# Fourth chunk: the third softmax group takes the slots of the first behind the softmax turns; two GpSimd memsets trade places

## The chip, the cores and the metric

The kernel runs on one NeuronCore of a Trainium2 chip (trn2), the seven other cores idle. The metric is device time in microseconds (us) of one execution. Before the change the median of three runs is 240.81 us (240.27 to 241.5). Smaller is better.

## The reference

Sinkhorn-sorted block attention, followed by a feed-forward layer with the activation h cos(h). Cut to what matters:

```python
# q, k, v: (4, 8, 768, 64); sort_net: (4, 8, 8, 8); w_in: (512, 2048); w_out: (2048, 512)
P = sort_net
for _ in range(5):
    P = exp(P - P.max(-1)); P = P / P.sum(-1); P = P / P.sum(-2)   # (+1e-9 in both sums)
k_sorted = einsum('bhij,bhjcd->bhicd', P, k_blocks)                # 8 blocks of 96 tokens
v_sorted = einsum('bhij,bhjcd->bhicd', P, v_blocks)
s = q_blocks @ k_sorted.T / 8                                      # per block of 96 tokens
attn = softmax(s) @ v_sorted
x = attn.transpose(0, 2, 1, 3).reshape(3072, 512)
h = x @ w_in
out = (h * cos(h)) @ w_out                                         # (3072, 512)
```

## The kernel before, in words

**Tiling.** The 3072 tokens are worked in eight chunks of 384 tokens, n = 0 to 7. A chunk is half a batch entry: four blocks of 96 tokens, which the code calls u = 0 to 3 and this text calls groups. "Fourth chunk" is n = 3, and its "first" and "third" groups are u = 0 and u = 2. The number n also says which buffer of a pair is used: `q_turned[n % 2]`.

**Steps of a group.** `qk n u` makes the scores of all eight heads on TensorE (PE; line 535), from the turned queries and the sorted keys: `kP0` for n = 1, `kP1` for n = 2 and 3, `kPg` from n = 4 on. `mx` takes row maxima off on VectorE (DVE; lines 572, 581). `ex` is the exponential on ScalarE (ACT; line 586), into one of three buffers `p_buf`. `pd` turns (transposes) the probabilities by a DMA on SyncE's queue (SP; line 598) into a tile `pT`; this is the softmax turn. `av` multiplies them with the sorted values on PE (line 617), with a column of ones that gives the softmax sums. `xn` takes the reciprocal of the sums and scales on DVE (lines 627, 629). The result is turned once more into the chunk's tile `xT`, by a DMA on SP (`xd`, line 638) or by PE (`xp`, line 646) and a copy on ACT or DVE.

**The layer.** When all four groups are in `xT`, `up` multiplies with `w_in` (line 661; a call of two 128-column tiles of `w_in` is eight matmuls), `ga` makes h cos(h) by a sine on ACT and a product on DVE (lines 671, 678) and `dn` multiplies with `w_out` (line 694). The `dn` calls of a chunk are laid between the attention steps of the next chunks, where they fill PE. `oc` copies results out of PSUM, `st` stores them by SP.

**Other steps near the change.** `vg` makes sorted values of batch entries 2 and 3 on PE (line 517) and `e vg` copies them out. `qd` turns a chunk's queries by SP (line 439). `z_k g part` is a memset on GpSimd (POOL; line 342) that zeroes one half (64 rows) of one of four slots of a key tile: `z_k 1 2` zeroes rows 64 to 127 of slot 0 of `kP1` (64x768), `z_k 2 1` rows 0 to 63 of slot 2 of `kPg` (64x1536). Before `z_k 1 2` may write, the copy `ksw 1 0` (SP, line 476) must have read that half of slot 0, since it moves it into slot 1. The scores of chunk 2, `qk 2 ...`, read all four slots of `kP1`. `ld_q`, `ld_kg` and `ld_vg` (lines 285, 270, 274) are loads that POOL issues. `v1` makes sorted values of batch entry 1 (line 508); `b_sum`, `b_inv` belong to the Sinkhorn rounds (lines 358, 386).

**What sets the order.** The list `PLAN` is the program order, written out by hand: each string is a call, each call issues instructions on fixed engines, and every engine and queue works through its own in that order (the schedule is manual, so nothing is moved). Waits come from the data that instructions share and from buffers: a name such as `B0` or `C1` at the end of a call is the PSUM pool in which its result lies until it is read. The lines ahead of the change in the fourth chunk:

```python
"pd 3 1", ..., "st 1 2 S", "pd 3 2", "e vg 40 4 A", "pd 3 0", ..., "qd 4", ..., "pd 3 3", "st 2 1 S",
```

So SP turns the groups in the order 1, 2, 0, 3, with the store `st 1 2` behind the first and `qd 4` ahead of the last.

Of the kernel before, what the change touches and what calls it, by code (L numbers as in the profile page):

```python
# [53 lines left out]
    "ex 1 2 0", "ld_q 2 0", "av 1 1 B0", "b_norm 1", "pp 1 2 C0", "dn 0 2 3", "xp 1 0 B2", "qd 2",  # L54
    "b_ci 1", "e pp 1 2 A", "ksw 1 0", "z_k 1 3", "xp 1 3 B1", "xn 1 1", "dn 0 2 0", "b_exp 1",
    "e xp 1 3 V", "av 1 2 B0", "xn 1 2", "xp 1 1 C0", "ld_q 3 2", "v1 40 8 B1", "e xp 1 1 A", "ld_kg 1 2",
    "e xp 1 0 A", "ld_kg 0 2", "dn 0 2 1", "z_k 2 1", "xp 1 2 B0", "e v1 40 8 V", "b_sum 1 C0",
    "e xp 1 2 A", "z_k 1 2", "qk 2 0 0 B2", "ld_q 3 0", "v1 48 8 B1", "b_inv 1", "qk 2 1 0 C0",
    "oc 0 2 V 0", "mx 2 0 0", "e v1 48 8 A", "mx 2 1 0", "up 1 0 2 0 384 B0", "up 1 4 2 0 384 B1",
    "b_norm 1", "ga 1 0 2 0 384", "up 1 6 2 0 384 B2", "up 1 14 2 0 384 B0", "ga 1 4 2 0 384", "st 0 1 S",  # L60
    "qk 2 0 1 C1", "up 1 10 2 0 384 B1", "ga 1 6 2 0 384", "up 1 12 2 0 384 B2", "ld_q 3 1", "mx 2 0 1",
    "ld_q 3 3", "ga 1 14 2 0 384", "ga 1 10 2 0 384", "v1 8 8 C0", "up 1 8 2 0 384 B0",
    "up 1 2 2 0 384 B1", "b_ci 1", "ga 1 12 2 0 384", "ld_vg 2 6", "e v1 8 8 V", "v1 24 8 C1",
# [18 lines left out]
    "dn 2 1 1", "dn 2 1 3", "dn 2 1 2", "mx 3 0 1", "pd 3 1", "mx 3 3 2", "vg 40 4 B0", "ld_q 5 0",  # L82
    "ex 3 0 0", "st 1 2 S", "pd 3 2", "e vg 40 4 A", "pd 3 0", "ld_q 5 3", "vg 48 4 B1", "dn 2 0 0",
    "oc 2 1 V 0", "vg 24 8 B2", "e vg 48 4 A", "dn 2 0 3", "av 3 1 B1", "vg 0 8 B0", "ex 3 3 0",
    "dn 2 2 3 C1", "e vg 24 8 A", "av 3 0 B2", "z_ones 1", "oc 2 0 A 0", "vg 36 4 C0", "e vg 0 8 A",
    "xn 3 1", "dn 2 2 1", "av 3 2 B0", "xn 3 0", "vg 8 8 B1", "qd 4", "dn 2 2 2", "xn 3 2", "e vg 36 4 A",
    "pd 3 3", "st 2 1 S", "av 3 3 B0", "xn 3 3", "e vg 8 8 A", "dn 2 2 0", "oc 2 2 A 0", "xp 3 1 B2",
    "e xp 3 1 V", "vg 32 4 C0", "xd 3 0", "qk 4 0 1 B0", "e vg 32 4 A", "xp 3 3 B1", "vg 16 8 B2",
    "xd 3 2", "e xp 3 3 V", "qd 5", "mx 4 0 1", "qk 4 1 1 C1", "qk 4 1 0 C0", "mx 4 1 1", "e vg 16 8 A",
    "up 3 4 2 0 384 B1", "up 3 6 2 0 384 B2", "mx 4 1 0", "up 3 0 2 0 384 B0", "ga 3 4 2 0 384",  # L90
    "qk 4 0 0 C1", "up 3 2 2 0 384 B1", "ga 3 6 2 0 384", "ga 3 0 2 0 384", "up 3 12 2 0 384 B2",
    "ga 3 2 2 0 384", "up 3 8 2 0 384 B0", "up 3 10 2 0 384 B1", "ga 3 12 2 0 384", "up 3 14 2 0 384 B2",
# [682 lines left out]
```

## Time and profile before

| | |
|---|---|
| median of 3 runs | 240.81 us (240.27 to 241.5) |
| the profiled execution's own time | 240.12 us |
| its span, first to last instruction | 238.3 us |
| PE busy | 229.6 us, 96% |
| VectorE / ScalarE / GpSimd busy | 174.0 / 147.9 / 73.6 us |
| mean granted TensorE clock | 0.997 |

The profile has a page of totals and views of the trace. In the timeline a row is: start, duration (us), engine, line, operation, out<-in and shapes, a count, and in brackets the idle time of the engine ahead of it with what ended it. PE is the matmul itself, PEld its weight load, which runs ahead beside PE. An SPq row is the issuing of a DMA, not its transfer. Matmuls overlap by about 0.2 us, so the distance from start to start tells more than the durations do. In the chain of waits (the work that ended last, followed back) a row is start, duration, what. In the view of DMA issues the last number is the time from the start of an issue to landing.

### The profile page before, as it was taken

The numbers are of one execution on the slowest core, as the hardware profiler recorded it, in microseconds if no ns is written. First come the engines' busy times: TensorE is split into PE (matmuls) and PEld (weight loads), VectorE is DVE, ScalarE is ACT, GpSimd is POOL, SyncE is SP. The second block draws the span as 40 slices with busy tenths as digits, with TensorE's granted clock in tenths as the row PEclk, the third lists the DMA queues.
The fourth block names the chain that finished last, engine by engine and source line by source line (L and its number), as shares of the span: only waits on it lengthen the run. The fifth ranks groups of instructions, "written<-read, shape, count | busy, mean of one in ns | idle before, by whom it ended". The sixth has DMA issues, their size and how long they took to land.

```text
span 238.3 us, 5223 instructions
## 1 busy us (share of the span) xinstructions
PE 229.6 (96%) x2127; PEld 148.3 (62%) x2127; DVE 174.0 (73%) x301; ACT 147.9 (62%) x202; POOL 73.6 (31%) x82
## 2 busy tenths in 40 slices
PE   8998998999999999999899999999999999999994
PEld 5787888966666565655565665555565555555543
DVE  2489967698879975796598888777989967715422
ACT  2346666766487967778486945783777387706420
POOL 8149599730942299930045000000000000000000
PEclk9999999999999999999999999999999999999998
DMA  5999999999999986979669346015731592331202
GB/s 67 232 188 224 200 188 125 157 183 156 200 193 199 178 183 142 154 48 161 162 87 114 57 95 149 12 23 112 192 91 28 139 184 44 94 96 66 110 37 95
DMA packets 67767, 30.78 MB, mean 129 GB/s; under 512 B 57248, under 2 KB 63264, under 8 KB 67488
## 3 DMA queue, kind: packets, MB, share of 16 engines
q0 software_dynamic: 26080, 13.63, 43.5%
q1 hardware_dynamic: 41296, 16.75, 31.1%
q8 instruction: 16, 0.26, 0.4%
q10 hardware_dynamic: 368, 0.07, 0.1%
q14 instruction: 7, 0.06, 0.1%
HBM read 27.27 MB, written 6.29 MB: 141 GB/s over the span
## 4 chain that ended last, share of the span: by engine, by line
PE 76%; DMA 9%; DVE 5%; POOL 4%; ACT 2%; issue 1%; SPq 1%; POOLq 0%; DVEq 0%; ACTq 0%
PE h L661 33%; PE o L694 28%; PE idle L347 4%; DMA w_in_t<-in_moe_w_in_dram 4%; PE sc L535 3%; PE av L617 3%; DMA pT<-p_buf 2%; DMA xT<-xn 2%; SPq L598 1%; DMA kP<-kP 1%; DVE kPg L369 1%; POOL vperm L491 1%; PE vs L517 1%; PE ks L467 1%; PE vs L499 1%
## 5 line engine op out<-in xcount | busy, mean ns | idle before, releaser
L694 PE MATMUL o<-w_out_t,gall 128*128 128x512 bf16 (+2 forms) x400 | 93.6, 370 | 0.1
L661 PE MATMUL h<-xT,w_in_t 128*128 128x384 bf16 (+1 forms) x576 | 86.8, 308 | 1.4 <-DMA w_in_t<-in_moe_w_in_dram 0.7
L678 DVE TENSOR_TENSOR gall<-c,h 128x768 bf16<-128x768 f32 x64 | 60.2, 951 | 25.3 <-ACT c L671 24.8
L671 ACT ACTIVATE c<-h,half_pi 128x768 f32<-128x768 f32 x64 | 57.3, 901 | 28.6 <-PE h L661 27.9
L661 PEld LDWEIGHTS <-w_in_t 128*128 128x128 bf16 x576 | 53.9, 98 | 31.1 <-issue 0.8
L694 PEld LDWEIGHTS <-gall 128*128 128x128 bf16 x400 | 36.2, 98 | 31.1 <-issue 0.4
L491 POOL COPY vperm<-kv 128x1536 bf16<-128x1536 bf16 (+1 forms) x10 | 28.3, 2848 | 10.1 <-PE sc L535 8.7
L586 ACT ACTIVATE p_buf<-s 96x768 bf16<-96x768 f32 x32 | 26.7, 842 | 6.4 <-DVE s L581 3.7
L572 DVE TENSOR_REDUCE mx<-sc 96x4 f32<-96x384 f32 (+1 forms) x39 | 28.1, 719 | 2.5 <-PE sc L535 2.5
L581 DVE TENSOR_TENSOR s<-sc,mx 96x384 f32<-96x384 f32 (+1 forms) x33 | 24.3, 736 | 2.3
L285 POOL DMA_DIRECT2D q_mem<-in_q_dram x24 | 18.5, 779 | 18.9 <-DMA q_turned<-q_mem 18.9
L629 DVE TENSOR_TENSOR xn<-av,r 96x512 bf16<-96x512 f32 x32 | 22.0, 686 | 1.1
L347 PE MATMUL idle<-warm 128*128 128x256 bf16 x109 | 17.4, 296 | 2.3 <-DVE warm L308 1.0
L249 ACT COPY kv<-o 128x512 f32<-128x512 f32 (+1 forms) x13 | 7.2, 557 | 15.6 <-PE o L694 15.6
L347 PEld LDWEIGHTS <-warm 128*128 128x128 bf16 x109 | 10.8, 108 | 5.4 <-DVE warm L308 1.0
L627 DVE RECIPROCAL r<-av 96x8 f32<-96x8 f32 x32 | 6.4, 201 | 10.3 <-PE av L617 9.9
L535 PEld LDWEIGHTS <-q_turned 128*128 128x128 bf16 x112 | 9.7, 100 | 4.5 <-issue 0.5
L249 ACT COPY xT<-xps 128x384 bf16<-128x384 bf16 x9 | 4.2, 479 | 12.3 <-PE xps L646 12.3
L671 ACT ACT_TABLE_LOAD x8 | 10.3, 1283 | 0.1
L617 PEld LDWEIGHTS <-pT 96*128 96x128 bf16 (+1 forms) x160 | 7.6, 101 | 4.0 <-DMA pT<-p_buf 1.4
L249 ACT CAST vS<-vs 96x512 bf16<-96x512 f32 x12 | 6.9, 585 | 5.0 <-PE vs L499 3.6
L249 ACT CAST pair<-vs 96x512 bf16<-96x512 f32 (+1 forms) x11 | 8.0, 746 | 3.2 <-PE vs L517 3.2
(103 smaller groups left out, 207.6 us busy)
## 6 DMA issues: line engine op xcount, KB each, us to landing
out_dram<-kv SPq DMA_DIRECT2D x14, 256.0 KB, 2.4
q_mem<-in_q_dram POOLq DMA_DIRECT2D x24, 96.0 KB, 3.6
out_dram<-o_s SPq DMA_DIRECT2D x9, 256.0 KB, 2.5
w_in_t<-in_moe_w_in_dram POOLq DMA_DIRECT2D x4, 512.0 KB, 11.5
w_out_t<-in_moe_w_out_dram POOLq DMA_DIRECT2D x4, 512.0 KB, 7.4
kv<-in_k_dram POOLq DMA_DIRECT2D x2, 768.0 KB, 8.1
kv<-in_v_dram POOLq DMA_DIRECT2D x2, 768.0 KB, 10.1
kv<-in_v_dram POOLq DMA_DIRECT2D x6, 256.0 KB, 11.0
```

The lines of the kernel that those rows point to most:

```text
L249: A.copy(dst, src)
L285: G.dma_start(out=q_mem[:, n % 2].rearrange("p (i h d) -> p i h d", i=IC, h=H)[:, i], in_=q[b].rearrange("h (i c) d -> i c h d", c=blk)[ih ...
L347: nc.tensor.matmul(idle[:], warm[:], warm[:, :1].to_broadcast([128, 256]), start=True, stop=True)
L491: G.tensor_copy(dst, src)
L572: V.reduce_max(m[:], scv, axis=AX.X)
L581: V.tensor_tensor(dst, scv, m.to_broadcast([blk, w, H2, blk]), op=ALU.subtract)
L586: A.activation(p[:, :, :blk], s_t.pop((n, u)).rearrange("p z a c -> p (z a) c"), AF.Exp, scale=scale)
L629: V.tensor_tensor(x[:], avv[:, :, :, :D], r.to_broadcast([blk, 2, H2, D]), op=ALU.mult)
L661: nc.tensor.matmul(hv[f], w_in_t[:, kk, (f0 + f) * 128:(f0 + f + 1) * 128], x_of(n)[:, kk, lo:hi], start=(kk == 0), stop=(kk == KC - 1))
L671: A.activation(cc, hh, AF.Sin, bias=half_pi[:, 0:1])
L678: V.tensor_tensor(dst, cc, hh, op=ALU.mult)
L694: nc.tensor.matmul(out_ps[key][:], gall[:, g_at(n, f), ts * 128:(ts + 1) * 128], w_out_t[:, f, c], start=(parts[key] == 1 and f == fs[0]), ...
```

## The change

In the fourth chunk, `av 3 0` and `av 3 2` trade places, and with them `xn 3 0` and `xn 3 2`, and `xd 3 0` and `xd 3 2`. The PSUM pools stay with the places: the first of the two uses B2 and the second B0, as before. So the order of `av` goes from 1, 0, 2, 3 to 1, 2, 0, 3. Further up, while chunk 1 is in the attention, `z_k 1 2` is put ahead of `z_k 2 1`. No call is added or taken away. (The other lines of the diff are the same calls wrapped differently.)

```diff
-    "e xp 1 0 A", "ld_kg 0 2", "dn 0 2 1", "z_k 2 1", "xp 1 2 B0", "e v1 40 8 V", "b_sum 1 C0",
-    "e xp 1 2 A", "z_k 1 2", "qk 2 0 0 B2", "ld_q 3 0", "v1 48 8 B1", "b_inv 1", "qk 2 1 0 C0",
+    "e xp 1 0 A", "ld_kg 0 2", "dn 0 2 1", "z_k 1 2", "z_k 2 1", "xp 1 2 B0", "e v1 40 8 V", "b_sum 1 C0",
+    "e xp 1 2 A", "qk 2 0 0 B2", "ld_q 3 0", "v1 48 8 B1", "b_inv 1", "qk 2 1 0 C0", "oc 0 2 V 0",
...
-    "dn 2 2 3 C1", "e vg 24 8 A", "av 3 0 B2", "z_ones 1", "oc 2 0 A 0", "vg 36 4 C0", "e vg 0 8 A",
-    "xn 3 1", "dn 2 2 1", "av 3 2 B0", "xn 3 0", "vg 8 8 B1", "qd 4", "dn 2 2 2", "xn 3 2", "e vg 36 4 A",
+    "dn 2 2 3 C1", "e vg 24 8 A", "av 3 2 B2", "z_ones 1", "oc 2 0 A 0", "vg 36 4 C0", "e vg 0 8 A",
+    "xn 3 1", "dn 2 2 1", "av 3 0 B0", "xn 3 2", "vg 8 8 B1", "qd 4", "dn 2 2 2", "xn 3 0", "e vg 36 4 A",
     "pd 3 3", "st 2 1 S", "av 3 3 B0", "xn 3 3", "e vg 8 8 A", "dn 2 2 0", "oc 2 2 A 0", "xp 3 1 B2",
-    "e xp 3 1 V", "vg 32 4 C0", "xd 3 0", "qk 4 0 1 B0", "e vg 32 4 A", "xp 3 3 B1", "vg 16 8 B2",
-    "xd 3 2", "e xp 3 3 V", "qd 5", "mx 4 0 1", "qk 4 1 1 C1", "qk 4 1 0 C0", "mx 4 1 1", "e vg 16 8 A",
+    "e xp 3 1 V", "vg 32 4 C0", "xd 3 2", "qk 4 0 1 B0", "e vg 32 4 A", "xp 3 3 B1", "vg 16 8 B2",
+    "xd 3 0", "e xp 3 3 V", "qd 5", "mx 4 0 1", "qk 4 1 1 C1", "qk 4 1 0 C0", "mx 4 1 1", "e vg 16 8 A",
```

4 rows, old and new, of the table PLAN are left out of this document.

## The prediction, made before the result was known

> **What bounds the kernel now.** I read the page first, for the engine that fills the span, and its slices.
>
> ```profile
> PE 229.6 (96%) x2127; PEld 148.3 (62%) x2127; DVE 174.0 (73%) x301; ACT 147.9 (62%) x202; POOL 73.6 (31%) x82
> ```
>
> TensorE is busy for 229.6 of 238.3 us, so a change that removes no matmul can win only where PE stands still. The list of who waited for whom says where, and the chain of waits whether such a place sets the end. Two places belong to the edits. In the first, between 56 and 65 us, the chain leaves PE and runs through a copy of keys and GpSimd's queue, and comes back to PE with the scores of chunk 2:
>
> ```profile
> 56.05 3.32 DMA kP<-kP
> ...
> 62.08 1.39 POOL kPg L342
> ...
> 63.52 0.74 POOL kP L342
> ...
> 64.31 0.32 PE sc L535 x2
> ```
>
> The reader is to see that the 1.39 us of `z_k 2 1` stand on the chain ahead of `z_k 1 2`, though the scores read only what `z_k 1 2` zeroes. In the second place the chain leaves PE for a softmax turn:
>
> ```profile
> 109.41 4.64 DMA pT<-p_buf
> ```
>
> This is `pd 3 0`, the third turn of chunk 3, which lands at 109.41 + 4.64 = 114.05; `av 3 0`, second of its chunk on PE, waits for it. Elsewhere the chain is matmuls nearly throughout, with short DMA turns that themselves begin at a PE result. Between the two places PE hardly ever rests, as the view of stretches shows for 60 to 92 us (length, then PE's busy time):
>
> ```profile
> 60.00:92.00 32.00, 31.59 (x304) 20.25 (x302) 25.55 (x48) 23.34 (x36) 20.08 (x18) 1.00 1.03 180
> ```
>
> With 31.59 us of 32 busy, time won at the first place should be kept by what follows.
>
> **Edit one, the two memsets.** The timeline there:
>
> ```profile
> 59.51 0.73 POOL L342 MEMSET kP<- 64x768 f32 x1 [9.25 <-DMA kP<-kP]
> ...
> 62.05 1.42 POOL L342 MEMSET kPg<- 64x1536 f32 x1
> ...
> 63.15 0.68 DVE L251 CAST vS<-vs 96x512 bf16<-96x512 f32 x1
> ...
> 63.52 0.73 POOL L342 MEMSET kP<- 64x768 f32 x1
> 63.54 0.35 PE L358 MATMUL sk<-E,kPg 128*128 128x8 f32 x2
> ...
> 63.74 0.48 ACT L249 COPY xT<-xps 128x384 bf16<-128x384 bf16 x1 [0.41 <-PE xps L646]
> 63.94 0.21 DVE L386 RECIPROCAL rr<-sk 128x8 f32<-128x8 f32 x1
> ...
> 64.21 2.34 POOL L285 DMA_DIRECT2D q_mem<-in_q_dram  x3
> 64.31 0.32 PE L535 MATMUL sc<-kP,q_turned 128*128 128x192 bf16 x2 [0.41 <-POOL kP L342]
> ...
> 64.47 0.40 PE L508 MATMUL vs<-kPg,vperm 128*128 128x64 bf16 x8
> ...
> 64.70 0.33 PE L535 MATMUL sc<-kP,q_turned 128*128 128x192 bf16 x2
> ...
> 64.87 5.36 PE L661 MATMUL h<-xT,w_in_t 128*128 128x384 bf16 x32
> ```
>
> The bracket says that PE stood 0.41 us for `z_k 1 2`. How early can that memset run? It must wait for the copy `ksw 1 0`, issued by SP at 59.14 and landing 3.6 us later:
>
> ```profile
> 59.14 0.69 SPq L476 DMA_DIRECT2D kP<-kP  x1
> ```
>
> ```profile
> kP<-kP SPq DMA_DIRECT2D x1, 192.0 KB, 3.6
> ```
>
> That is 62.74. The other copy landed at 56.05 + 3.32 = 59.37 and its memset began at 59.51, so 0.14 us later; `z_k 1 2` can begin at 62.88, not at 62.05. In the trace of before its start and the start of the scores are 64.31 - 63.52 = 0.79 apart; so the zeros allow the scores at 62.88 + 0.79 = 63.67. PE itself reaches them about 0.15 behind the small fp32 pair, estimated from the same pair at its earlier place, ahead of `av`:
>
> ```profile
> 57.62 0.28 PE L358 MATMUL sk<-E,kPg 128*128 128x8 f32 x2
> ...
> 57.77 0.42 PE L617 MATMUL av<-vS,pT 96*128 96x65 bf16 x8
> ```
>
> So 63.54 + 0.15 = 63.69, and the memset is just in time: the first scores gain 64.31 - 63.69 = 0.62. What is late next? Taking 0.06 from a finished instruction to the one it releases (the memset's 63.52 + 0.73 = 64.25 against 64.31): `v1 48 8`, 0.16 behind the scores, would go at 63.85, and its pool B1 is free when the cast at 63.15 ends, 63.83 + 0.06 = 63.89. `qk 2 1 0` would follow 0.23 later, at 64.12, but its pool C0 is read by the reciprocal `b_inv` until 63.94 + 0.21 = 64.15, so 64.21. The first `up` comes 0.17 behind, at 64.38; its `xT` is copied by 63.74 + 0.48 = 64.22. Against 64.87 that is **0.49 us** won. Bounds: 0 from below if something else holds the scores to 64.31, 0.62 from above if both pools let go early.
>
> [...]
>
> What the edit pushes back: POOL now idles from 62.07 to 62.88, so `z_k 2 1` runs at about 63.6 to 65.0 and everything POOL issues behind it comes about 0.8 later: `ld_q 3 0`, `3 1`, `3 3`, then three `ld_vg`, up to a fourth that waits for an older load until 71.32 anyway:
>
> ```profile
> 71.32 0.53 POOL L274 DMA_DIRECT2D kv<-in_v_dram  x1 [3.14 <-DMA pair<-in_k_dram]
> ```
>
> ```profile
> 81.21 1.40 SPq L439 DMA_TRANSPOSE q_turned<-q_mem  x1
> ```
>
> ```profile
> q_mem<-in_q_dram POOLq DMA_DIRECT2D x1, 96.0 KB, 11.0
> ```
>
> The last query load (issued until 64.21 + 2.34 = 66.55, 11.0 to landing) is there before 77.6, by 78.4 after the change, and `qd 3` uses it at 81.21: nearly 3 us of cover. POOL stood 3.14 us ahead of 71.32, which takes up the 0.8, so the last `ld_vg`, and the copies `vp` that need all of them, keep their time. The first user of `z_k 2 1` itself is the copy `ksw 2 1`, behind `qd 3` in the plan. I cost all of this at nothing; if the cover were gone, PE would wait by what is missing, at most the 0.8.
>
> **Edit two, the fourth chunk.** SP turns groups 1, 2, 0, 3, but PE asks in the order 1, 0, 2, 3:
>
> ```profile
> 108.05 2.60 SPq L598 DMA_TRANSPOSE pT<-p_buf  x2
> ...
> 112.13 1.03 PE L694 MATMUL o<-w_out_t,gall 128*128 128x512 bf16 x4
> ...
> 112.83 1.24 SPq L598 DMA_TRANSPOSE pT<-p_buf  x1
> 114.10 0.32 PEld L617 LDWEIGHTS <-pT 96*128 96x128 bf16 x8 [1.44 <-DMA pT<-p_buf]
> 114.11 0.43 PE L617 MATMUL av<-vS,pT 96*128 96x65 bf16 x8 [0.95 <-DMA pT<-p_buf]
> 114.16 0.53 SPq L709 DMA_DIRECT2D out_dram<-o_s  x1
> ...
> 114.60 1.03 PE L694 MATMUL o<-w_out_t,gall 128*128 128x512 bf16 x4
> ...
> 115.46 0.42 PE L617 MATMUL av<-vS,pT 96*128 96x65 bf16 x8
> 115.53 2.52 SPq L638 DMA_TRANSPOSE xT<-xn  x2
> ...
> 117.03 0.42 PE L617 MATMUL av<-vS,pT 96*128 96x65 bf16 x8
> ...
> 119.78 4.06 PE L661 MATMUL h<-xT,w_in_t 128*128 128x384 bf16 x24
> ```
>
> ```profile
> pT<-p_buf SPq DMA_TRANSPOSE x1, 3.7
> ```
>
> ```profile
> pT<-p_buf SPq DMA_TRANSPOSE x1, 3.1
> ```
>
> (The first is `pd 3 2`, the second `pd 3 3`.) From 114.60 to 115.46, four `dn` matmuls take 0.86 from start to start; without a wait `av` would have begun at 112.13 + 0.86 = 112.99. So the stall is 114.11 - 112.99 = 1.12, more than the 0.95 of the bracket, which counts from a modelled end.
>
> After the change that place holds `av 3 2`, whose turn landed at 108.05 + 3.7 = 111.75, more than 1 us ahead. The 1.12 falls away. The next place, now `av 3 0`, would begin at 115.46 - 1.12 = 114.34; its turn lands at 114.05, good from 114.11: 0.23 to spare. The third, `av 3 3`, would begin at 117.03 - 1.12 = 115.91, but its turn lands at 112.83 + 3.1 = 115.93, so it begins at 115.99. What is left of the gain is 117.03 - 115.99 = **1.04 us**. That small wait is what is late next.
>
> The moved `xd` calls: SP is free after the store at 114.16 + 0.53 = 114.69. `xd 3 2` goes then instead of at 115.53, `xd 3 0` behind it, 1.26 later (half of 2.52), at about 116.0, and lands 2.3 later:
>
> ```profile
> xT<-xn SPq DMA_TRANSPOSE x2, 2.3
> ```
>
> That is 118.3; the first `up` of the chunk, at 119.78 before, would come at 118.74. Cover 0.4 us; each tenth by which that turn is slower than this costs a tenth. No instruction is added, and `qd 5` behind the two on SP goes earlier with them. Bounds of this edit: 1.12 if `pd 3 3` lands a tenth sooner; below nothing if the `xT` turn is slow (the third rival).
>
> **Sum.** 0.49 + 1.04 = 1.53 us: the profiled execution of 240.12 would become 238.59. That execution is a little under the lowest run shown (240.27); the median is 240.81, so I forecast 240.81 - 1.53 = 239.28, about **239.3 us**, 0.64% faster. A measurement of this kernel can tell about 0.5% (1.2 us, so 239.6 or 242.0) from no change; the forecast is only just past that.
>
> **Rivals.** First, the memset swap buys nothing: the second memset could have run early as it was, and something else holds the scores to 64.31. For it: PE's bracket of 0.41 is small, and two pools come free only at 63.83 and 64.15. Against: the chain of waits runs without a gap through both memsets. Then only 1.04 is left: 239.8. Chance 0.18.
>
> Second, edit two is swallowed: PE gains at 112.99 and then waits for `xd 3 0`, at the first `up`. It needs a landing at 119.7, 3.7 us after issue, which is what `pd 3 2` took. For it: the two turns start closer behind `qd 4` and `pd 3 3`, which are still moving until 115.9. Against: the same two took 2.3 in this same place, with `pd 3 3` in flight at 115.53 as well. Then 0.49 is left: 240.3. Chance 0.14.
>
> Third, slower: that turn takes 4.64 us like `pd 3 0`. `xd 3 0` then lands at 120.64, the `up` begins at 120.70 instead of 119.78, 0.92 late, and with the 0.49 of edit one the whole is 0.43 slower: 241.2. It decides from a landing at about 120.2, where loss and gain are even. For it: `pd 3 0` shows that a turn can take so long behind a store and another turn, and `st 2 1` is issued right ahead here. Against: neither of the two was slow at this place before, with the same store in front of them. Chance 0.05.
>
> **How the numbers follow.** 0.63 is left for the forecast. Its own range goes from 0.62 + 1.12 = 1.74 won (239.1) to 1.04 + 0.2, where the first edit gives half, (239.6); half a microsecond of spread between runs on the quick side gives a low end of 238.5. The high end takes in the first and second rivals: 240.4. Faster by over 0.5%: nine tenths of the forecast and a little of the first rival, 0.59. Slower by over 0.5% needs more than the third rival's price: 0.04. The rest, 0.37, is within.
>
> **What would show it.** In the changed profile: POOL's 64x768 memset starts near 62.9, ahead of the 64x1536 one near 63.6; the scores of chunk 2 start near 63.7 with no wait for POOL, and the first `up` near 64.4. All in chunk 3 about 0.5 earlier; no wait of 0.95 for a `pT` turn ahead of the second `av`; at most a tenth ahead of the fourth. The ups of chunk 3 start about 1.5 earlier than 119.78. It is wrong if the scores still start at 64.3, if a wait for `xT` stands ahead of those ups, or if the half microsecond of the first edit is gone before 105 us, for instance at the first `av` of chunk 2, whose turn (issued about 79 us) shares the DMA engines with POOL's late loads.

## The result, and the profile after

The changed kernel takes 238.95 us (median of 20 runs, 237.58 to 241.4), the kernel before 240.2 us in the same comparison (20 runs, 238.51 to 244.57). The ratio is 0.9942, 95% interval 0.992 to 0.9965: 1.4 us won (0.8 to 1.9), where 1.53 was forecast. The forecast of 239.3 us was counted from 240.81, the median of three runs; in this comparison the kernel before takes 240.2. The profiled execution took 238.48 us instead of 240.12.

The page of the changed kernel, engine totals:

```profile
PE 228.0 (96%) x2108; PEld 148.0 (63%) x2127; DVE 171.7 (73%) x301; ACT 147.9 (62%) x202; POOL 73.6 (31%) x82
```

PE's busy time is lower by 1.6 us though no matmul was taken out; of 2127 matmuls this trace has the records of 2108, so the sum is not evidence. Starts of instructions are.

**The first place.** The timeline of the changed kernel:

```profile
61.61 0.73 POOL L342 MEMSET kP<- 64x768 f32 x1 [0.69 <-DMA kP<-kP]
...
62.40 1.38 POOL L342 MEMSET kPg<- 64x1536 f32 x1
...
62.99 0.35 PE L358 MATMUL sk<-E,kPg 128*128 128x8 f32 x2
...
63.20 0.32 PE L535 MATMUL sc<-kP,q_turned 128*128 128x192 bf16 x2
...
63.80 0.65 PE L661 MATMUL h<-xT,w_in_t 128*128 128x384 bf16 x3
```

The small memset now ends at 62.34, and the scores follow 0.21 behind the small fp32 pair (before: 0.77), with no bracket for POOL. From that pair to the first `up` it is 0.81 us; before it was 64.87 - 63.54 = 1.33. So 0.52 us of waiting is gone here (forecast 0.49). The whole place is also 0.55 earlier than in the trace of before, from work ahead of any edit. The large memset begins only when the other has ended (62.40 after 62.34), though they write different rows, as in the trace of before (63.52 after 62.05 + 1.42 = 63.47). So the first rival, by which the second memset could have run early as it was, has nothing for it here either. The chain of waits no longer leaves PE at this place:

```profile
62.98 0.17 PE xps L646 x4
63.15 0.19 PE sk L358 x2
63.34 0.18 PE sc L535 x2
63.52 0.23 PE vs L508 x8
63.97 5.20 PE h L661 x32
```

**What is given back.** Further down the same chain leaves PE where it did not before:

```profile
77.89 4.58 DMA pT<-p_buf
82.51 0.43 PE av L617 x8
...
89.06 2.32 DMA xT<-xn
91.52 10.56 PE h L661 x64
```

That is `pd 2 0`, the turn for the first `av` of chunk 2. It lands at 82.47. In the trace of before the same `av` began at 83.33, 18.46 after the first `up` of chunk 1; here it is 82.51 - 63.80 = 18.71. So 0.25 us is lost again in this execution. Whether the edit brings that about is taken up further down.

**The second place**, PE in the changed kernel's timeline, fourth chunk:

```profile
110.54 0.42 PE L617 MATMUL av<-vS,pT 96*128 96x65 bf16 x8
...
111.24 1.03 PE L694 MATMUL o<-w_out_t,gall 128*128 128x512 bf16 x4
112.11 0.42 PE L617 MATMUL av<-vS,pT 96*128 96x65 bf16 x8
...
113.45 0.42 PE L617 MATMUL av<-vS,pT 96*128 96x65 bf16 x8
...
115.03 0.43 PE L617 MATMUL av<-vS,pT 96*128 96x65 bf16 x8
...
117.79 0.49 PE L661 MATMUL h<-xT,w_in_t 128*128 128x384 bf16 x2
```

From the first `av` to the second it is 1.57 us; before it was 2.69 (111.42 to 114.11). The 1.12 of waiting is gone, no wait for `xT` stands ahead of the `up`, and that `up` comes 119.78 - 117.79 = 1.99 earlier. Of this 0.89 was already there ahead of chunk 3 (112.13 against 111.24), so edit two gave 1.10. SP's queue and the landings of the moved turn:

```profile
112.02 1.23 SPq L598 DMA_TRANSPOSE pT<-p_buf  x1
113.35 0.53 SPq L709 DMA_DIRECT2D out_dram<-o_s  x1
113.97 2.50 SPq L638 DMA_TRANSPOSE xT<-xn  x2
```

```profile
xT<-xn SPq DMA_TRANSPOSE x1, 2.3
```

`xd 3 0`, the second of the pair, is issued at about 115.2 (1.25 behind the first) and lands 2.3 later, at 117.5. The `up` at 117.79 had 0.3 to spare; 0.4 was forecast.

The account of the trace: 0.55 from above any edit, 0.52 from edit one, 0.25 given back, 0.07 won back on the way to chunk 3 (so 0.89 there), 1.10 from edit two, and 0.32 lost at the first `up` of chunk 4 (145.32 against 143.65, so 1.67 where 1.99 stood). There the last turn into `xT` takes 2.29 us in both traces, but is issued 1.17 behind the last `av` instead of 0.83. That leaves 1.67; the spans differ by 1.6 (238.3 and 236.7).

### The profile page after: what moved, and what is told of

Same layout as the page of the kernel before. It is cut to its first block, busy times and chain, and to the rows that moved or that the text cites. A ratio compares the mean times of both kernels' runs of the same rounds, so it can differ in the third digit from the quotient of the medians.

```text
span 236.7 us, 5204 instructions
## 1 busy us (share of the span) xinstructions
PE 228.0 (96%) x2108; PEld 148.0 (63%) x2127; DVE 171.7 (73%) x301; ACT 147.9 (62%) x202; POOL 73.6 (31%) x82
## 4 chain that ended last, share of the span: by engine, by line
PE 75%; DMA 15%; POOL 4%; ACT 2%; DVE 2%; issue 1%; SPq 0%; POOLq 0%
PE h L661 32%; PE o L694 30%; DMA kv<-in_v_dram 5%; DMA w_out_t<-in_moe_w_out_dram 3%; PE av L617 3%; DMA kPg<-kPg 3%; PE sc L535 3%; POOL vperm L491 2%; DMA xT<-xn 2%; DMA pT<-p_buf 2%; PE vs L517 2%; PE idle L347 1%; DVE xn L629 1%; PE xps L646 1%; PE pps L607 1%
## 5 line engine op out<-in xcount | busy, mean ns | idle before, releaser
L694 PE MATMUL o<-w_out_t,gall 128*128 128x512 bf16 (+2 forms) x381 | 90.9, 370 | 2.3 <-DMA w_out_t<-in_moe_w_out_dram 1.4
L347 PE MATMUL idle<-warm 128*128 128x256 bf16 x109 | 16.7, 290 | 1.5 <-DVE warm L308 1.0
L535 PE MATMUL sc<-kPg,q_turned 128*128 128x192 bf16 x80 | 10.0, 246 | 0.0
```

The lines of the kernel that those rows point to most:

```text
L347: nc.tensor.matmul(idle[:], warm[:], warm[:, :1].to_broadcast([128, 256]), start=True, stop=True)
L535: nc.tensor.matmul(out, q_turned[n % 2][:, c:c + 128], keys, start=True, stop=True)
L694: nc.tensor.matmul(out_ps[key][:], gall[:, g_at(n, f), ts * 128:(ts + 1) * 128], w_out_t[:, f, c], start=(parts[key] == 1 and f == fs[0]), ...
```

## The experiments

There were two theories at the start. The prediction's: both waits were real, and each edit gives its term. The rival: edit one buys nothing over many executions, and edit two is all of the gain. Later a third question came up: why one softmax turn is so slow.

### Each edit alone

Edit one alone:

```diff
-"z_k 2 1", ..., "z_k 1 2", "qk 2 0 0 B2",
+"z_k 1 2", "z_k 2 1", ..., "qk 2 0 0 B2",
```

> Only the two GpSimd memsets trade places; the fourth chunk stays as before. Theory: the scores of chunk 2 no longer wait for the zeros and the first up comes about 0.5 us sooner behind the small fp32 pair than before (0.8 us instead of 1.3 us from that pair to the up). But the first av of chunk 2 then meets a softmax turn that lands with the last value load, whose end does not move, so 0.2 to 0.3 us of it are given back there; the whole is 0.2 to 0.4 us faster than before. The 0.95 us wait ahead of the second av of chunk 3 stays. Rival (the swap buys nothing): the up still comes 1.3 us behind the pair and the whole does not change.

Measured: 240.26 us against 239.87, ratio 1.0027 (0.9995 to 1.006). A gain of 0.49 us (0.2%) lies outside that interval. In the profile the wait is gone, as it should be (0.82 us from the pair to the `up`), and nothing is given back at the first `av` of chunk 2, against the expectation (18.46 from the `up`):

```profile
62.73 0.73 POOL L342 MEMSET kP<- 64x768 f32 x1 [0.61 <-DMA kP<-kP]
63.52 1.38 POOL L342 MEMSET kPg<- 64x1536 f32 x1
```

Edit two alone, the memsets as before:

```diff
-"av 3 0 B2", ..., "av 3 2 B0", "xn 3 0", ..., "xn 3 2", ..., "xd 3 0", ..., "xd 3 2"
+"av 3 2 B2", ..., "av 3 0 B0", "xn 3 2", ..., "xn 3 0", ..., "xd 3 2", ..., "xd 3 0"
```

> Only the fourth chunk: av, xn and xd of groups 0 and 2 trade places; the memsets stay as before. Theory: the PE wait for the zeros stays (0.4 us), the wait ahead of the second av of chunk 3 goes, a wait of about 0.1 us comes ahead of the fourth; from the dn behind the first av to the first up 6.6 us instead of 7.65, and the whole is 1.0 us faster than before, two thirds to three quarters of what both edits bring. Rival (swallowed): the first up of chunk 3 waits for the last xT turn and the distance stays at 7.65 us.

Measured: 239.04 us, ratio 0.9958 (0.9923 to 0.9994): 1.0 us. First to second `av` is 1.57 as in the changed kernel. So it is in all seven profiles with the new order of `av`; in the seven with the old order it is 2.29 to 2.69. The profile of edit two alone also shows why edit one paid so little. Its memsets stand in the old order:

```profile
61.88 1.42 POOL L342 MEMSET kPg<- 64x1536 f32 x1
63.35 0.73 POOL L342 MEMSET kP<- 64x768 f32 x1
...
64.00 0.35 PE L358 MATMUL sk<-E,kPg 128*128 128x8 f32 x2
64.21 0.33 PE L535 MATMUL sc<-kP,q_turned 128*128 128x192 bf16 x2
```

The reader is to see that PE came to the fp32 pair at 64.00, 0.46 later than in the trace of before, while the memset ended at 64.08, even a little sooner. The scores follow 0.21 behind the pair, as in the new order: nobody waited. Which of the two is late differs from execution to execution.

### The place of the zeros

The memset of the scores put later, not sooner: three query loads, which POOL issues, stand between the two memsets.

```diff
-"z_k 2 1", "xp 1 2 B0", ..., "z_k 1 2", ..., "ld_q 3 0", ..., "ld_q 3 1", ..., "ld_q 3 3"
+"z_k 2 1", "ld_q 3 0", "ld_q 3 1", "ld_q 3 3", ..., "z_k 1 2"
```

> The kernel before with the suspected wait made large: the three query loads that GpSimd issues behind the 64x768 memset go ahead of it, so that the zeros come 2.3 us later. Theory (what is lost at this place is lost at the end but for what the first softmax turn of chunk 2 gives back): PE waits 2.3 to 2.9 us ahead of the scores of chunk 2, and the whole is 1.9 to 2.6 us slower than before, ratio 1.008 to 1.011. Rival (the loads, which end near 82 us, set the start of chunk 2's attention, so lost time before is hidden): the first av of chunk 2 comes less than 1 us later and the whole is under 1 us slower.

Measured: 242.94 us against 240.0, ratio 1.0093 (1.0055 to 1.0131), 2.2 us slower. The timeline, PE and POOL:

```profile
64.63 0.35 PE L358 MATMUL sk<-E,kPg 128*128 128x8 f32 x2
66.93 0.33 PE L535 MATMUL sc<-kP,q_turned 128*128 128x192 bf16 x2 [1.94 <-POOL kP L342]
```

```profile
63.74 2.36 POOL L285 DMA_DIRECT2D q_mem<-in_q_dram  x3
66.14 0.73 POOL L342 MEMSET kP<- 64x768 f32 x1
```

PE stood 2.05 us there (pair to `up` 2.86 instead of 0.81), and none of it was given back at the first `av` of chunk 2 (18.46). The time rose by 2.2 us (1.3 to 3.1). So time lost at this place is not hidden by what follows. How nearly one for one it counts is not shown, because the profiled execution (244.15 us, one of the longer ones) has a second wait: the first `up` of chunk 2 stood 1.67 us for a turn into `xT` that took 4.1 us. Of edit one it is not the mechanism that failed, but the size.

### Given back at chunk 2

The changed kernel without the last of POOL's value loads, 256 KB of batch entries 2 and 3; nothing else is moved.

```diff
-"ld_vg 5 6",
```

> The changed kernel without the last of the six value loads of batch entries 2 and 3 (256 KB), so a sixth of those values is wrong. Theory: the first softmax turn of chunk 2 took 4.6 us in the changed kernel because that load was still moving; without it the turn lands about 3 us after its issue, the first av of chunk 2 does not wait, and the up of chunk 2 comes 0.3 to 0.5 us sooner counted from the up of chunk 1; the whole about 0.3 us faster than the changed kernel, so 1.7 us faster than before. Rival: the turn is slow for a reason of its own queue (the query turn behind it), still takes over 4 us, and nothing changes.

Measured: 238.95 us, ratio to before 0.9961 (0.9928 to 0.9994), the same as the changed kernel within what can be told. In the profile `pd 2 0` landed in 2.9 us and the first `av` of chunk 2 waited for nothing (18.47 from the `up`). That fits the cause named in the prediction, POOL's late loads, but does not show it: another thing differed too, below. In chunk 3 of this profile the fourth `av` came 1.94 us behind the third instead of 1.57, a wait for its turn at the place where the prediction had put a tenth.

### Why the turn of group 0 is slow

In the trace of before `pd 3 0` took 4.64 us. Edit two works round it; what makes it slow? First, its place in SP's order: `pd 3 0` ahead of `pd 3 2`, `av` in the old order.

```diff
-"pd 3 2", "e vg 40 4 A", "pd 3 0",
+"pd 3 0", "e vg 40 4 A", "pd 3 2",
```

> The kernel before, with its order of av kept (1, 0, 2, 3), but the two softmax turns on SP put in that order: group 0 before group 2. Theory: what stalls PE is that the turn asked for second is issued third. With the turns exchanged the second av does not wait, as in the changed kernel. But group 0 has its exponential 1 us later than group 2, so SP begins the pair about 0.65 us later and the last turn lands later by as much: av of group 3 waits 0.5 to 0.7 us, and only 0.4 to 0.5 us of the 1.04 is won; 0.2% faster than before. Rival (the turn of group 0 is slow whatever its place): it still lands 4 us or more after issue, near 113.5, the second av waits 0.5 us or more, and nothing is won.

Measured: 239.93 us, 1.0015 (0.9979 to 1.0051). The turn took longer still, the turn of group 2, now behind it, took 4.6 us as well, and the second `av` waited again (2.50 behind the first). So the delay does not belong to group 0's data. The chain of waits, then PE:

```profile
108.19 5.18 DMA pT<-p_buf
```

```profile
110.92 0.42 PE L617 MATMUL av<-vS,pT 96*128 96x65 bf16 x8
113.42 0.43 PE L617 MATMUL av<-vS,pT 96*128 96x65 bf16 x8 [0.77 <-DMA pT<-p_buf]
```

Then the store ahead of the pair (`st 1 2`, 256 KB), moved up to behind `ksw 2 0`: in the kernel before, in the changed kernel, and with edit two alone.

```diff
+"ksw 2 0", "st 1 2 S",
-"pd 3 1", ..., "st 1 2 S", "pd 3 2",
```

> The kernel before, order of av kept, with one edit: the store st 1 2 (256 KB, ready since 92 us) leaves its place between the softmax turns of groups 1 and 2 on SP and goes ahead of all four, behind the key copy near 94 us. Theory: group 0's turn is late (4.6 us from issue to landing) because the store, and the turns that pile up behind it, are still moving. Without it the turns of chunk 3 land in 2.8 to 3.0 us as those of chunk 4 do, the turn of group 0 about 111.9 on the clock of the profile before, ahead of the 112.99 at which PE asks for it: the wait ahead of the second av goes without any change of order, and the whole is 1.1 us faster than before. Rival (two turns issued back to back are slow in themselves in this stage): group 0 still takes over 4 us, PE still waits 0.9 us, and the time is that of before.

> The changed kernel with the same store moved ahead of the turns. Theory: both cures act on the same wait, so they do not add: only the wait of about 0.1 to 0.15 us ahead of the fourth av goes as well, and the time is 0.1 us under the changed kernel, 1.2 us under before (ratio 0.994 to 0.995). Rival (they add, since the turns also hold something else): 1 us or more under the changed kernel.

> As the last one, but with the two memsets in their old order; the difference of the two is the memset swap alone once more. Theory after the first runs: the wait for the zeros is there only in executions in which PE comes early against GpSimd (0 to 0.5 us, no wait where the small fp32 pair comes 0.6 us or more behind the start of the 64x768 memset), and what it costs is partly given back at the first softmax turn of chunk 2; so the two times differ by 0.0 to 0.3 us, within what can be told. Rival (my forecast's step): the kernel with the old order is 0.5 us slower in every execution.

Measured, as ratios to before: 0.9993 (0.9959 to 1.0026), 0.9971 (0.9938 to 1.0004) and 0.9962 (0.993 to 0.9994). The first turn of the pair, group 2's, came down from 3.7 to 2.7 or 2.8 us; group 0's stayed at 4.7 to 4.9. The store slowed the other turn, not this one. The last two runs differ by the memset swap alone: 0.9971 with it, 0.9962 without, so here too the times show no gain from it. In the last of the three the first `up` of chunk 2 waited 1.49 us for `xT`, and its chain of waits has

```profile
89.44 3.76 DMA xT<-xn
```

where the trace of before has 2.31 for the same turn. The store that had been moved is issued only at 93.65, when this turn has landed (93.20).

Then the query turn `qd 4`, issued right behind `pd 3 0`: moved behind `pd 3 3` in the kernel before and in the changed one, and in the latter also `qd 3` behind `pd 2 3`.

```diff
-"pd 3 0", ..., "qd 4", ..., "pd 3 3",
+"pd 3 0", ..., "pd 3 3", "qd 4",
```

> The kernel before, order of av kept, store in its old place; only the query turn qd 4 goes behind the softmax turn of group 3 on SP instead of ahead of it, so that it no longer follows the turn of group 0 at once. Theory after the store was cleared: a softmax turn with a query turn (twice its size) right behind it shares the DMA engines with it and lands 4.5 to 5 us after its issue instead of 3; so the turn of group 0 now lands near 3 us, ahead of the 112.99 at which PE asks, the wait ahead of the second av goes, and group 3's turn, which now has the query turn behind it, takes 4 us or more but is issued earlier and is in time: 1.1 us faster than before (ratio 0.995 to 0.996). Rival (group 0's turn is slow for a reason of its own, whatever follows): still 4.6 us, the wait stays, no gain.

> The changed kernel with that same move of qd 4. Theory: the wait that the change took away cannot be won twice; only the wait of 0.1 us or so ahead of the fourth av can go, so the time is that of the changed kernel within 0.2 us (ratio to before 0.993 to 0.996). Rival: the query turn also delays the xT turns behind it, and the first up of chunk 3 then waits: slower than the changed kernel by 0.3 us or more.

> As the last one, and in chunk 2 the query turn qd 3 goes behind the second softmax turn instead of right behind the first. Theory: the first turn of chunk 2 then lands 3 us after its issue even when PE comes early, so that the first av never waits (it waited 0.25 us in the changed kernel's profile, 0.5 and 0.9 us in two others) and the first edit keeps what it wins: 0.2 to 0.4 us under the changed kernel on the average, hardly to be told in the times, plain in the trace (18.46 us from the first up of chunk 1 to the first av of chunk 2). Rival (the loads slow that turn, not the query turn): it still takes 4 us or more where PE comes early.

Measured: 1.0008 (0.997 to 1.0046), 0.9966 (0.9927 to 1.0004), 0.9976 (0.9938 to 1.0013). Group 0's turn took 4.6, 4.6 and 4.7 us. It is not the query turn either. In the last two the first `up` of chunk 3 came 7.70 and 7.84 us behind the first `av` instead of 7.25: the loss that the rival of the second run named, but by another way, since the scores ahead of the `up` waited for a copy on ScalarE and not for `xT`. In chunk 2 of the third run `pd 2 0` still took 4.2 us without the query turn right behind it, as the rival there said. The first `av` did not wait (18.45 from the `up`): the turn landed at 83.6, and PE came to it at 83.78.

What was left was a line in the DMA view. While the slow turn of the kernel before is in flight (109.4 to 112 us), two queues move one packet each beside the transfers of the program:

```profile
q1 hardware_dynamic: 1487, 0.37, 82.1%
q8 instruction: 1, 0.02, 2.7%
q14 instruction: 1, 0.01, 0.8%
```

The columns are packets, MB and their time as a share of 16 engines. The profile gives the kind of both queues as instruction, so they were taken to fetch instructions; no view shows what the packets hold. On the page of before q8 stands with all its packets:

```profile
q8 instruction: 16, 0.26, 0.4%
```

That is 16 KB each; TensorE has 2127 matmuls and as many weight loads, so if q8 is TensorE's it is about 266 of them for a packet. That it is TensorE's was not shown: no view names the engine that a queue serves. In the four turns of chunk 4 (133.7 to 139 us), which took 2.9 us at the median, there is no such packet.

To move that packet, if it is TensorE's, the kernel before was given more TensorE instructions at its beginning: 18 idle matmuls of 256 columns became 36 of 128.

```diff
-    def w(times, pool):
+    def w(times, pool, c=256):
...
-        for _ in range(times):
+        for _ in range(times * 256 // c):
...
-"w 8 B0", ..., "w 5 C0", ..., "w 5 C1",
+"w 8 B0 128", ..., "w 5 C0 128", ..., "w 5 C1 128",
```

> The kernel before, its order unchanged, with 18 of its 109 idle matmuls, all ahead of 12 us, each cut into two of half the columns: the same TensorE time, 18 matmuls and 18 weight loads more. Fetch theory: the turn of chunk 3's group 0 is late because a packet of queue q8 (16 packets for 4,250 TensorE rows, so one in some 266) falls into its flight. Before, that packet ran at 111.6 and the turn, issued at 109.41, landed at 114.05, 2.45 behind it; in six profiles the turn in flight landed 2.4 to 3.2 behind such a packet. 36 rows more bring it forward by about 1.5 us, to 110.1, so the turn lands at about 112.6, in 3.2 us instead of 4.6, the 1.12 us in front of the second av of chunk 3 goes (first to second av 1.57 instead of 2.69), and the time falls by about 1.0 us, to a ratio of 0.996, with no call moved; the turn of chunk 2's group 0 lands in under 3.0 us; the packet of 95.5 moves to 92.6, close to the last xT turn of chunk 2 (lands 92.26), and may make that late by some tenths. Rival, place: what is late is the second turn of a pair with a query turn behind it, whatever is fetched; the turn keeps 4.6 us, first to second av stays at 2.5 to 2.7, ratio 1.000. Rival, the other queue: the q14 packet at 110.3 is what delays it; that one does not move, and the turn still lands at 114.0.

Measured: 241.94 us against 240.29, ratio 1.0064 (1.003 to 1.0098), slower. The turn took 4.6 us as before, as both rivals said, but that does not decide against the fetch theory, because the packet at chunk 3 did not move: it runs at 113.0, 0.1 behind the first `av` of that chunk (before 111.6, 0.2 behind). The q14 packet did not move against the turn either (1.0 behind its issue, before 0.9). It lies in the flight of `pd 3 0` in all fourteen profiles, so no run separates it from the q8 packet there. In chunk 2 the fetch theory had `pd 2 0` land in under 3.0 us; it took 3.7, though the packet ran only 0.2 behind its issue. And the packet that was at 95.5 ran at 90.0 here, in the flight of chunk 2's `xT` turns. DMA view of that run, 90 to 91 us, and PE's timeline:

```profile
q8 instruction: 1, 0.02, 9.8%
issues: line engine op xcount, KB each, median us to landing
xT<-xn SPq DMA_TRANSPOSE x2, 3.7
```

```profile
93.91 1.30 PE L661 MATMUL h<-xT,w_in_t 128*128 128x384 bf16 x7 [0.96 <-DMA xT<-xn]
```

The second and third of those turns took 2.3 us before (no instruction packet there) and 4.0 and 3.4 here, and the first `up` of chunk 2 came 93.91 - 84.12 = 9.79 behind the first `av` instead of 9.07. So 0.7 us is lost here. Another 0.8 of this profile stands ahead of 65 us, which is within the spread from execution to execution; whether the added instructions cost time there is open.

## Why the prediction was right, and where it was off

**The time.** 1.53 us forecast, 1.4 measured (0.8 to 1.9). The sum holds within that interval, but not because each of its terms did: edit two carries the gain, and that the sum came out so near is in part luck.

**Edit two, 1.04 forecast.** 1.10 in the trace, 1.0 alone in the comparison of times (0.1 to 1.8). The mechanism was right: the group that takes the place had its turn long landed, the two `xT` turns went earlier and took 2.3 us, nothing was late at the `up`. At most a tenth was forecast ahead of the fourth `av`; it began 115.03 - 113.45 = 1.58 behind the third (before 1.57), so there was none to speak of in this trace; 0.37 stood there in the one without the last load. The second and third rival, a late `xT` turn, did not come about at this place.

**Edit one, 0.49 forecast: the term that was mis-sized.** The working took the 0.41 of one bracket and the 63.54 of one fp32 pair as if they were the kernel's. They are one execution's. The distance from the pair to the first `up` of chunk 1 is 0.81 to 0.82 when nobody waits. In the profiles with the old order (the kernel before, edit two alone, and five others without a late memset) it was 1.33, 0.81, 1.17, 0.82, 1.00, 1.03 and 1.16: waits of 0.52, 0, 0.36, 0, 0.19, 0.22 and 0.35, a mean of 0.23. The trace that the prediction read happened to be the largest of the seven. In the six profiles with the new order it was 0.81 or 0.82 every time. So the edit does what was said, for about half the price in the traces. In the times no gain of it is shown at all: edit one alone came out 0.27% slower (-0.05% to 0.6%), an interval that leaves out even a gain of 0.23 us (0.1%), and the pair of runs with the store moved shows none either. The first rival (the swap buys nothing) was wrong on the mechanism and nearer on the amount. A smaller reading was off as well: the scores come 0.21 behind the small pair when nobody waits, not the 0.15 estimated, and the rest of the way to the `up` is shorter by about as much (0.60 instead of 0.69).

**Given back.** The prediction named the place, the first `av` of chunk 2, at which the half microsecond could go, and counted nothing for it. It was 0.25 in the changed kernel's profile. But the runs do not tie it to the edit: of the six profiles with the new order of the memsets only that one shows it (18.45 to 18.47 us from the `up` to the `av` in the others), while two of the eight with the old order lost more there (19.01 and 19.37). The cause that the prediction gave, late loads of POOL, is not excluded. Over fourteen profiles the landing of `pd 2 0` goes with an instruction packet (next but one section), but in twelve of them the last value load also landed 0.6 to 0.9 us ahead of it; in the other two, the run without that load and the one with late zeros, the turn took 2.9 and 2.8 us. In the run with more instructions, where the packet came early and the turn still took 3.7, the load fits better than the packet; the edit that would separate the two was not made.

**Costed at nothing.** The later query loads and the later `z_k 2 1` delayed no one: `qd 3` went at 79.29, 1.40 behind `pd 2 0`, and no wait for `kPg` appeared. Right.

**What stays open.** Why `pd 3 0` takes 4.6 to 5.2 us. Its place in the order, the store, the query turn and the count of TensorE instructions ahead of it were each changed, and none of them made it fast. That an instruction packet delays it, q8's or q14's, is argued, not shown: in chunk 3 neither could be moved. One more thing in the trace of before fits it. The q8 packet took about 1.1 us of one engine (2.7% of 16 engines over 2.6 us), and from 112.5 to 113.5, ahead of the landing at 114.05, the DMA view has only 39 small packets of the turns left, 9 GB/s, as if one engine were behind; in the run without the last load, whose `pd 2 0` landed at 81.2, the rate falls from 260 GB/s to nothing within 0.2 us, by 80.7. The view does not name the engines. No version tried beats the changed kernel: with the store moved up as well it takes 238.87 us (237.62 to 240.4), which can't be told from it.

## What to carry to other kernels

A wait read from one profile is one draw: where two engines arrive at about the same time, take the wait from several executions, or count it at half. The wait for `pd 3 0`, about a microsecond in the trace that was read, stood in every profile with the old order (0.7 to 1.1 us). Where a transfer's landing can't be made sooner, let work that is already there go first, and move the steps behind the two along with it. And a turn far from the edit can take over a microsecond longer in one execution than in another: `pd 2 0`, issued at about 79 us, took 3.7 us in the trace of before and 5.2 in the kernel before with the store moved, though that store goes out only near 94 us. So a difference of half a per cent in one profile may have nothing to do with the edit.

## What the runs showed of the hardware that was not expected

**A softmax turn's landing goes with an instruction packet.** For `pd 2 0` the distance from issue to the nearest q8 packet (read in steps of a tenth of a microsecond) ran from 0 to 2.5 us in fourteen profiles, and the landing came 2.6 to 3.5 behind the packet in all of them. Three profiles, in order: chunk 2 without the last load, the changed kernel, the kernel before with the store moved.

```profile
q8 instruction: 1, 0.02, 3.5%
...
pT<-p_buf SPq DMA_TRANSPOSE x1, 2.9
```

```profile
q8 instruction: 1, 0.02, 2.5%
...
pT<-p_buf SPq DMA_TRANSPOSE x1, 4.6
```

```profile
q8 instruction: 1, 0.02, 2.1%
...
pT<-p_buf SPq DMA_TRANSPOSE x1, 5.2
```

The packets lay 0.3, 1.9 and 2.5 us behind the issue (78.6, 79.8, 82.4 against 78.31, 77.89, 79.88). For `pd 3 0` the landing was 2.0 to 2.6 behind the packet. The `xT` turns of chunk 2 took 2.3 or 2.4 us in eleven profiles. In the other three one or two of them took 3.4 to 4.1, and these are exactly the three where a q8 packet fell into their flight (90.0, 91.1 and 94.1 us); none of POOL's loads was moving then. One of these three is the run with the added idle instructions; in the other two the packet came early without a count being changed, so it is open what moved it in the first. Whether packet and turn delay each other or both wait for something else, no run separates.

**The two memsets on GpSimd, on different rows, ran one behind the other.** The first rival had the second able to run early. They took 0.73 and 1.4 us, with 0.04 to 0.06 between the end of one and the start of the other by the profile, in either order.

**Executions scatter by up to 2.4 us** in the start-up alone: the fp32 pair ahead of chunk 2's scores began between 62.71 and 65.14 us in twelve profiles whose work up to there is the same but for the order of the two memsets.
